# Blocks of 128 groups in all four planes, longer store rows, one load for the last V groups, and an order read from strings

## The chip, the cores and the metric

The kernel runs on one core of one Trainium2 chip. The metric is the device time of one execution in microseconds. The kernel before takes 323.43 us (median of 3 runs, 322.58 to 326.46). Profiles are of one execution, and their times count from the start of its span.

## The reference, cut to what matters

```python
q, k, v: [8, 8, 576, 64]                  # batch, heads, tokens, head_dim
q_d, k_d, v_d = means over 4 neighbouring tokens (144 groups)
out_up = repeat(softmax(q_d @ k_d.T / 8) @ v_d, 4)        # pooled attention
out_local = softmax(q @ k.T / 8 where |i - j| < 4) @ v    # banded attention
x = (out_up + out_local) as [4608, 512]   # batch * token, head * head_dim
h = x @ w_in                              # [512, 2048]
out = (h - tanh(h)) @ w_out               # [2048, 512], float32
```

Token 4g + c of a batch is plane c of group g.

## The kernel before, in words

A pair is two heads of one batch: 32 pairs, four to a batch. For each pair the kernel loads k and q (`st`, line 366), v in five overlapping windows of 128 tokens (`vst`, line 390), and for some pairs v by groups (`v4`, line 400), casts and transposes them, makes the band scores (L657, L665) and the pooled scores (L671), which use 64 rows of PE for each head, exponentials on ACT, a mask on DVE or POOL, the outs (L725), a division (L742), a transpose back and a sum of the local and the pooled part (`join`, L760). Pooled v comes for pairs 0 to 11 from products of `vw` with a selecting matrix (`pool_v`, L458), for the others from `v4` by two additions on POOL (`pool_v4`, L440, L444). The last 16 groups of k and q of all heads of a batch come in loads of their own (`sr`, line 378).

The result of a batch lies in four tiles `xT` (one per pair) of [128, 3 x 576], by plane: column c x 144 + g of a batch's slot. The dense part takes the first 512 columns of a slot, which are planes 0 to 2 and 80 groups of plane 3, as block kb (`mm1`, L803: 16 x 4 products of 128 x 512). The last 64 columns, groups 80 to 143 of plane 3, are left over; those of two batches are taken together (`left1`, L829: 4 x 16 products of 128 columns; `left2`, L855). The second product is L883 for blocks 0 to 4, and for blocks 5 to 7 a scheme of seven products in place of eight (`product`, L1030) with sums of weights (L939) and of tokens (L965, on DVE or POOL). Stores (`store`, L919) take 128 columns of the block for each of four `ts`; where such a stretch crosses from one plane to the next, it is cut in two. One row of such a store is one token's 512 values, 2 KB; for the last block 256 values.

The order of the work is a planner's (`Plan.order`): operations carry a cost in ns, a priority and the banks of PSUM that they may take, and a simulated clock puts next what can start first. A string (`GIVEN`) names the engine where there is a choice. `Plan.emit` puts filler products (L1240, on a tile of zeros) into PE gaps before the first `h` of block 1. Instructions then stand on each engine in that order and start in it.

The moving operand of a left product, before:

```python
xT[dc].rearrange("p (b c) -> p b c", c=S)[:, s0:s0 + 2, 512:S]        # line 831
```

and the one product before whose moving operand takes columns with a step (`sums`, lines 611 and 622):

```python
sel = ident.rearrange("p (g j n) -> p n g j", j=NP, n=2)[:, :, :, j]   # every 8th column
T.matmul(pl[:, :, 128:G], rr[b % 2][:, c, :], sel, start=False, stop=c == 3, ...)
```

Of the kernel before, what the change touches and what calls it, by code (L numbers as in the profile page):

```python
# [14 lines left out]
class Plan:  # L15

    LAT = {"PE": 270, "ACT": 160, "DVE": 130, "POOL": 160, "SP": 50, "DMA": 1900,
           "DW": 1900}

    def __init__(self, given):
        self.ops = []
        self.given, self.choices = given, 0
        self.last_write = {}
        self.readers = {}
        self.users = {}  # L30
        self.place = {}

    def op(self, eng, ns, fn, reads=(), writes=(), pri=0, after=0.0, slack=0.0,
           port=False, opens=None, uses=(), choice=None, rows=128, share=0.4):
# [15 lines left out]
        names = set(uses)  # L50
        if opens and not isinstance(opens, list):
            opens = [opens]
        for o in opens or ():
            names.add(o[0])
        for n in names:
            self.users.setdefault(n, []).append(i)
        if choice:

            letter = self.given[self.choices]
            self.choices += 1  # L60
            named = [a[:4] for a in choice if a[0][0] == letter]
            choice = named or [a for a in choice if len(a) == 4]
        alts = {a[0]: a for a in choice} if choice else {eng: (eng, ns, fn, port)}
        self.ops.append(dict(alts=alts, deps=deps, pri=pri, after=after, slack=slack,
                             opens=opens, names=names, rows=rows, share=share,
                             what=(list(writes) + [None])[0]))
        return i

    def order(self):
        ops, n = self.ops, len(self.ops)  # L70
        users = [[] for _ in range(n)]
        left = [0] * n
        for i, o in enumerate(ops):
            left[i] = len(o["deps"])
            for d in o["deps"]:
                users[d].append(i)
        at = [o["after"] for o in ops]
        free, ready = dict.fromkeys(("PE", "ACT", "DVE", "POOL", "SP", "DMA"), 800.0), {}
        start, engine = [None] * n, [None] * n
        pending = {k: len(v) for k, v in self.users.items()}  # L80
        ends = {}
        bank_free = [0.0] * 8
        held = [None] * 8
        port_free = 0.0
        rows = 128
        self.held = []

        def make_ready(i):
            for eng in ops[i]["alts"]:
                ready.setdefault(eng, []).append(i)  # L90

        def seats(i):
            t, got, used = 0.0, [], set()
            for _, cs in ops[i]["opens"] or ():
                best = (float("inf"), None)
                for c in cs:
                    if any(held[b] is not None or b in used for b in c):
                        continue
                    best = min(best, (max(bank_free[b] for b in c), c), key=lambda x: x[0])
                if best[1] is None:  # L100
                    return float("inf"), None
                t = max(t, best[0])
                got.append(best[1])
                used.update(best[1])
            return t, got
        for i in range(n):
            if left[i] == 0:
                make_ready(i)
        for _ in range(n):
            best = None  # L110
            for eng, cand in ready.items():
                if not cand:
                    continue
                fr = free.get(eng, 0.0)
                if eng in ("DMA", "DW"):
                    i = min(cand, key=lambda i: (at[i], i))
                    now = max(fr, at[i])
                else:
                    now, i = None, None
                    eff = []  # L120
                    for c in cand:
                        t = max(at[c], seats(c)[0], fr)
                        if ops[c]["alts"][eng][3]:
                            t = max(t, port_free)
                        eff.append((t, c))
                    now = min(eff)[0]
                    if now == float("inf"):
                        continue
                    i = min((ops[c]["pri"], c) for t, c in eff if t <= now)[1]
                if best is None or now < best[0]:  # L130
                    best = (now, eng, i)
            if best is None:
                raise RuntimeError(f"no operation can be put next: {[(e, [(ops[c].get('what'), at[c], ops[c]['opens']) for c in cs[:6]]) for e, cs in ready.items()]} {held}")
            now, eng, i = best
            for other in ops[i]["alts"]:
                ready[other].remove(i)
            o = ops[i]
            _, ns, fn, port = o["alts"][eng]
            o["fn"], o["ns"] = fn, ns
            for (name, _), c in zip(o["opens"] or (), seats(i)[1] if o["opens"] else ()):  # L140
                self.place[name] = c
                for b in c:
                    held[b] = name
                self.held.append([name, c, now, None])
            start[i], engine[i] = now, eng
            if eng == "PE":

                if o["rows"] != rows:
                    ns += 60 if rows == 128 else 95
                rows = o["rows"]  # L150
            if eng == "DMA":

                ns *= 0.89 if now > 60000 else 0.82

                slow = max(0.0, free.get("DW", 0.0) - now)
                f = o["share"]
                ns = ns / f if ns <= f * slow else ns + (1 - f) * slow
            end = now + ns
            free[eng] = end
            if port:  # L160
                port_free = end
            for name in o["names"]:
                ends[name] = max(ends.get(name, 0.0), end + self.LAT[eng])
                pending[name] -= 1
                if pending[name] == 0:
                    for b in self.place[name]:
                        held[b] = None
                        bank_free[b] = ends[name]
                    for h in self.held:
                        if h[0] == name:  # L170
                            h[3] = ends[name]
            for u in users[i]:
                same = eng in ops[u]["alts"] and len(ops[u]["alts"]) == 1 and \
                    eng not in ("DMA", "DW")
                at[u] = max(at[u], end if same else end + self.LAT[eng] + ops[u]["slack"])
                left[u] -= 1
                if left[u] == 0:
                    make_ready(u)
        self.start, self.engine = start, engine
        return sorted(range(n), key=lambda i: (start[i], i))  # L180

    def emit(self, until=None, filler=None):
        order = self.order()
        stop = min([h[2] for h in self.held if h[0] == until], default=0.0)
        last = 600.0
        for i in order:
            o = self.ops[i]
            if filler and self.engine[i] == "PE" and self.start[i] <= stop:
                gap = self.start[i] - last
                if gap > 350:  # L190
                    busy = {b for _, c, s, e in self.held for b in c
                            if s < self.start[i] and e > last - 300}
                    rest = [b for b in range(7, -1, -1) if b not in busy]
                    if rest:
                        slow = 430 if self.start[i] < 6000 else 230
                        filler(rest[0], int(0.75 * gap / slow))
                last = self.start[i] + o["ns"]
            if o["fn"] is not None:
                o["fn"]()
# [3 lines left out]
def kernel(  # L203
# [49 lines left out]
    ]  # L253

    GIVEN = (
        "..A..D.DADA.PADDADPDD.AADD..D.DD.AA.DA.ADAA....ADAD..AA..P...AP.D..AP....DDPPPDD"
        "..D..A.A...PAAAPPPAADDD.DDDDAD.ADAD.A..PPPDDDAA...A.....DA..A.AA.PD.D..ADPDDAP.P"
        "D.PP..D.DDDDD.P..DP...DADP...P....A...D.PP..DPAAPP..P.D..AD..A..DD.PPD.PA..D.P.."
# [213 lines left out]
    def attention(p):  # L472
# [248 lines left out]
        def outs():  # L721
            po = at(oname)
            for hh in range(2):
# [6 lines left out]
                for i in range(2):  # L730
                    to(1, EP + 256 * i + 128, vp[s][:, hh, i, :], False, i == 1)
# [540 lines left out]
```

## Time and profile before

| What | Value |
|---|---|
| Timed runs (3) | 323.43 us median, 322.58 to 326.46 |
| Span of the profiled execution | 320.7 us |
| Clock of TensorE granted, mean | 1.000 |
| Products on PE | 2831 |
| DMA | 59.23 MB in 117205 packets, mean 185 GB/s |

The profile gives the span of its execution, from the first to the last instruction; what lies around it in a timed run is the difference to the median, 2.7 us. PE is the matmul engine, PEld its weight loads, DVE, ACT and POOL are the vector, scalar and GpSimd engines, SP issues most DMAs. A line as L829 is a line of the kernel. A product's length in the profile holds its way through the array, in which the next ones already run: the distance from one start to the next tells the rate.

### The profile page before, as it was taken

What the parts mean: (1) busy time and instruction counts of PE and PEld (TensorE: products, weight loads), DVE (VectorE), ACT (ScalarE), POOL (GpSimd) and SP (SyncE); (2) the same over time, 40 slices, a digit from 0 to 9 for tenths busy, and PEclk for the clock granted to TensorE, in tenths of its full rate; (3) what the DMA queues carried; (4) which work ended last, traced back from release to release, by engine and by line L of the source; (5) the groups of instructions that cost most, each with busy time, mean ns of one, the idle gap of its engine ahead of it and who ended that gap; (6) DMA issues with size and microseconds to landing.
All of it is one profiled execution on the core that took longest, in us unless ns stands there. A gap on an engine that the chain in (4) does not pass through costs nothing.

```text
span 320.7 us, 7553 instructions
## 1 busy us (share of the span) xinstructions
PE 309.1 (96%) x2831; PEld 181.0 (56%) x2831; DVE 255.3 (80%) x451; ACT 207.8 (65%) x372; POOL 156.8 (49%) x185
## 2 busy tenths in 40 slices
PE   7978999999999999999999999999899999999994
PEld 3654546554754545454655444545476667666783
DVE  5685997597888898679888999899999797656853
ACT  5884995588856776369745878579766852455210
POOL 7822664326267473537464735357794653511000
PEclk9999999999999999999999999999999999999999
DMA  8999999999999999999999999995452143200414
GB/s 218 275 219 227 279 185 247 289 277 304 240 232 274 236 210 246 224 255 195 245 222 177 269 237 251 232 223 112 94 92 57 35 49 93 67 0 3 130 36 131
DMA packets 117205, 59.23 MB, mean 185 GB/s; under 512 B 85008, under 2 KB 112592, under 8 KB 117168
## 3 DMA queue, kind: packets, MB, share of 16 engines
q1 hardware_dynamic: 111584, 52.17, 71.3%
q0 software_dynamic: 4896, 5.97, 10.0%
q10 hardware_dynamic: 688, 0.61, 0.6%
q8 instruction: 22, 0.36, 0.4%
q14 instruction: 15, 0.12, 0.1%
HBM read 43.65 MB, written 9.44 MB: 166 GB/s over the span
## 4 chain that ended last, share of the span: by engine, by line
PE 88%; DMA 7%; DVE 1%; SPq 1%; ACT 0%; POOL 0%; ACTq 0%; issue 0%; POOLq 0%
PE ps L803 34%; PE ps L883 22%; PE ps L1030 11%; DMA vst<-in_v_dram 6%; PE ps L725 5%; PE ps L829 5%; PE ps L855 4%; PE ps L657 3%; DMA sr<-in_q_dram 1%; PE ps L671 1%; PE ps L510 1%; PE ps L458 1%; PE ps L767 1%; PE ps L665 1%; SPq L366 1%; DVE xT L760 1%
## 5 line engine op out<-in xcount | busy, mean ns | idle before, releaser
L803 PE MATMUL ps<-xT,w_in_sb 128*128 128x512 bf16 x512 | 124.6, 379 | 0.0
L817 DVE TENSOR_TENSOR gT<-ps,u 128x512 bf16<-128x512 f32 x128 | 86.0, 684 | 21.2 <-ACT u L814 19.6
L814 ACT ACTIVATE u<-ps 128x512 f32<-128x512 f32 x128 | 76.1, 599 | 36.2 <-PE ps L803 33.6
L883 PE MATMUL ps<-w_out_sb,gT 128*128 128x512 bf16 x320 | 78.6, 379 | 0.0
L803 PEld LDWEIGHTS <-w_in_sb 128*128 128x128 bf16 x512 | 47.1, 98 | 47.3 <-issue 0.4
L883 PEld LDWEIGHTS <-gT 128*128 128x128 bf16 x320 | 29.2, 98 | 31.2
L444 POOL TENSOR_TENSOR vp<-v 128x256 bf16<-128x256 f32 x20 | 14.6, 730 | 58.7 <-PE ps L725 48.1
L676 ACT ACTIVATE E<-ps 128x912 bf16<-128x912 f32 x32 | 29.8, 931 | 17.8 <-PE ps L665 14.6
L1030 PEld LDWEIGHTS <-gT 128*128 128x128 bf16 x288 | 27.9, 98 | 7.5
L742 DVE TENSOR_TENSOR ln<-ps,r 128x768 bf16<-128x768 f32 x32 | 30.6, 956 | 0.9
L711 DVE TENSOR_TENSOR E<-E,mask 128x1152 bf16<-128x1152 bf16 x29 | 25.6, 882 | 4.4 <-ACT E L680 4.2
L502 POOL CAST qr<-st 128x512 bf16<-128x512 f32 x32 | 22.5, 713 | 9.3 <-DMA st<-in_q_dram 6.0
L440 POOL TENSOR_TENSOR v<-v 128x512 f32<-128x512 f32 x20 | 25.4, 1271 | 1.1
L725 PEld LDWEIGHTS <-E 128*128 128x128 bf16 x576 | 21.7, 97 | 6.1
L684 ACT ACTIVATE E<-ps 128x576 bf16<-128x576 f32 x32 | 20.9, 654 | 0.0
L583 ACT COPY kt<-kq 128x576 bf16<-128x576 bf16 x16 | 18.9, 1180 | 2.9 <-DVE kq L578 2.7
L593 POOL TENSOR_TENSOR half<-kq 128x576 f32<-128x576 bf16 x13 | 18.1, 1389 | 3.6 <-DVE kq L578 1.5
L725 PE MATMUL ps<-vw,E 128*128 128x65 bf16 x320 | 18.9, 193 | 0.0
L760 DVE TENSOR_TENSOR xT<-lT 128x336 bf16<-128x336 bf16 (+1 forms) x30 | 18.4, 655 | 0.0
L1030 PE MATMUL ps<-Tw,gT 128*128 128x256 bf16 x144 | 18.3, 273 | 0.0
L725 PE MATMUL ps<-vp,E 128*128 128x65 bf16 x256 | 18.1, 193 | 0.0
L1030 PE MATMUL ps<-w_out_sb,gT 128*128 128x256 bf16 x144 | 17.8, 273 | 0.0
(118 smaller groups left out, 434.9 us busy)
## 6 DMA issues: line engine op xcount, KB each, us to landing
vst<-in_v_dram SPq DMA_DIRECT2D x64, 160.0 KB, 4.8
st<-in_k_dram SPq DMA_DIRECT2D x32, 256.0 KB, 4.6
st<-in_q_dram SPq DMA_DIRECT2D x32, 256.0 KB, 4.6
v<-in_v_dram SPq DMA_DIRECT2D x14, 256.0 KB, 3.6
w_in_sb<-in_moe_w_in_dram POOLq DMA_DIRECT2D x4, 512.0 KB, 12.7
w_out_sb<-in_moe_w_out_dram POOLq DMA_DIRECT2D x4, 512.0 KB, 12.2
out_dram<-y SPq DMA_DIRECT2D x7, 256.0 KB, 3.8
out_dram<-y SPq DMA_DIRECT2D x7, 224.0 KB, 3.1
```

The lines of the kernel that those rows point to most:

```text
L440: eng.tensor_tensor(out=v2, in0=v4[s][:, :, :, 0:128], in1=v4[s][:, :, :, 128:256], op=ALU.add)
L502: (eng, ns, lambda dst=dst, src=src, fn=fn: fn(out=dst, in_=src), port)
L676: A.activation(out=E[s][:, :, E0:E0 + 456], in_=at(s1)[:, :, PS0:512], func=AF.Exp, scale=SCALE)
L711: eng.tensor_tensor(out=el, in0=el, in1=mask.unsqueeze(1).to_broadcast([128, 2, S]), op=ALU.mult)
L725: T.matmul(po[:, hh, 65 * n:65 * n + 65], E[s][:, hh, e:e + 128], vv, start=start, stop=stop)
L742: op("DVE", 960, lambda: V.tensor_tensor(out=ln[s].rearrange("p n (h d) -> p h n d", d=D), in0=blocks()[:, :, :, 0:64], in1=r[s].unsqueeze ...
L760: eng.tensor_tensor(out=dst, in0=src, in1=add, op=ALU.add)
L803: T.matmul(at(name)[:, 0, :], w_in_sb[:, dc, fc * 128:(fc + 1) * 128], xT[dc][:, c0:c0 + 512], start=(dc == 0), stop=(dc == N_DC - 1))
L814: op("ACT", 600, lambda: A.activation(out=u[us], in_=at(name)[:, 0, :], func=AF.Tanh), reads=[("hd", kb, fc)], writes=[("u", us)], pri=-1, ...
L817: op("DVE", 690, lambda: V.tensor_tensor(out=gT[g][:, fc, :], in0=at(name)[:, 0, :], in1=u[us], op=ALU.subtract), reads=[("hd", kb, fc), ( ...
L883: T.matmul(at(name)[:, 0, :], gT[g][:, fc, ts * 128:ts * 128 + 128], w_out_sb[:, fc, :], start=(fc == 0), stop=(fc == N_FF - 1))
L1030: T.matmul(dst, left[:, f, 128 * j:128 * j + 128], right[:, f, :], start=(first and e == 0 and f == 0 and (j == 0 or apart)), stop=(e == 1 ...
```

## The change

The blocks are cut otherwise: a block is now groups 0 to 127 of all four planes, and the left-over tokens of a batch are groups 128 to 143 of all four planes, which are the last 64 tokens. The moving operand of `mm1` becomes four runs of 128 columns; that of `left1` goes through the 16 groups and, for each, over the four planes, so that the 64 tokens come out in the order of the output. A store takes 128 groups of two planes at once: a row of it is two tokens, 4 KB (for the last block 2 x 1 KB), and none is cut at a plane's end. The last 16 groups of v of all eight heads of a batch come in one load `vr` and are pooled at once into `vpr`, in which a mask (`hsel`) leaves each head its own 16 rows; `v4`, `v2` and `vp` keep the first 128 groups alone, and `pool_v` has five products for six. The pooled scores read the rows of the second half at a shifted place (`w0`). The additions of `pool_v4` may now be on DVE too.

The planner is gone. `TURNS` gives the order of all operations, `ENGINES` the engine of each choice, `BANKS` the PSUM bank of each opening and `FILL` place, bank and number of the fillers (24 in all). Costs that stand in the calls of `op` are not used any more. ACT's table is loaded by a copy of one element at the start. Cut to its core:

```diff
-    def order(self):
...
+    def emit(self, filler):
+        n = len(self.ops)
+        turn = [self.number(self.turns[2 * i:2 * i + 2]) for i in range(n)]
...
+        for i in turn:
+            fn, deps, opens, names = self.ops[i]
...
+            if i in fill:
+                b, count = fill[i]
+                filler(b, count)
+            for name, sets in opens:
+                c = self.place[name] = sets[int(next(seats))]
...
+            if fn is not None:
+                fn()
...
     def load_v4(p):
-        vv = v[b, h0:h0 + 2].rearrange("h (g c) d -> g h (c d)", c=4)
-        for i in range(2):
-            load(770 if SOFT[p] else 450,
-                 lambda i=i: (nc.gpsimd if SOFT[p] else nc.sync).dma_start(
-                     out=v4[s][0:128 - 112 * i, :, i], in_=vv[128 * i:144 - 16 * (1 - i)]),
+        load(770 if SOFT[p] else 450,
+             lambda: (nc.gpsimd if SOFT[p] else nc.sync).dma_start(
+                 out=v4[s], in_=v[b, h0:h0 + 2].rearrange("h (g c) d -> g h (c d)", c=4)[0:128]),
...
+    def load_vr(b):
+        base = v[b, 0]
+        load(500, lambda: nc.sync.dma_start(out=vr[b % 2], in_=bass.AP(
+            tensor=base.tensor, offset=base.offset + 512 * D,
+            ap=[[S * D, H], [4 * D, 16], [1, 4 * D]])),
...
+    def pool_vr(b):
...
+        def spread(eng):
+            eng.tensor_tensor(out=vpr[b % 2], in0=vrp.unsqueeze(1).to_broadcast([128, H, D + 1]),
+                              in1=hsel.unsqueeze(2).to_broadcast([128, H, D + 1]), op=ALU.mult)
...
     def pool_v(p, seats):
-            for n, (i, t) in enumerate(((0, 0), (0, 1), (0, 2), (0, 3), (0, 4), (1, 4))):
-                T.matmul(pv[:, i, :], pick[:, n, :], vw[w][:, :, t, 0:D],
-                         start=n in (0, 5), stop=n in (4, 5))
+            for t in range(NT):
+                T.matmul(at(name)[:, 0, 0:2 * D], pick[:, t, :], vw[w][:, :, t, 0:D],
+                         start=t == 0, stop=t == NT - 1)
...
     def mm1(kb, fc):
-                         xT[dc][:, c0:c0 + 512], start=(dc == 0), stop=(dc == N_DC - 1))
+                         xT[dc][:, c0:c0 + S].rearrange("p (c g) -> p c g", c=4)[:, :, 0:128],
+                         start=(dc == 0), stop=(dc == N_DC - 1))
...
     def left1(m, e):
-                             xT[dc].rearrange("p (b c) -> p b c", c=S)[:, s0:s0 + 2, 512:S],
+                             xT[dc].rearrange("p (b c g) -> p b g c", b=NR, c=4)[:, s0:s0 + 2, 128:G],
...
     def left2(m):
-            row = out[(2 * m + (n + m) % 2) * S + 4 * (G - LEFT) + 3]
+            row = out[(2 * m + (n + m) % 2) * S + 512]
-                out=bass.AP(tensor=row.tensor, offset=row.offset, ap=[[4 * Dm, LEFT], [1, Dm]]),
+                out=bass.AP(tensor=row.tensor, offset=row.offset, ap=[[Dm, LEFT], [1, Dm]]),
...
-    def store(kb, ts, ys, j, half=None, queue="SP"):
+    def store(kb, half, ys, js=(0, 1), part=None, rows=(0, 128), queue="SP"):
...
+            row = out[kb * S + 4 * r0 + 2 * half + js[0]]
+            (nc.sync if queue == "SP" else nc.scalar).dma_start(
+                out=bass.AP(tensor=row.tensor, offset=row.offset + lo,
+                            ap=[[4 * Dm, n], [Dm, len(js)], [1, hi - lo]]),
+                in_=y[ys][r0:r1, js[0]:js[-1] + 1, lo:hi])
```

More of the change, by code (lines that the diff above doesn't have):

```diff
@@ L15, with __init__, op @@
 class Plan:
-    LAT = {"PE": 270, "ACT": 160, "DVE": 130, "POOL": 160, "SP": 50, "DMA": 1900,
-           "DW": 1900}
-    def __init__(self, given):
+    DIGITS = "0123456789ABCDEFGHIJKLMNOPQRSTUVWXYZabcdefghijklmnopqrstuvwxyz"
+    def __init__(self, turns, engines, banks, fill):
         self.ops = []
-        self.given, self.choices = given, 0
+        self.turns, self.engines, self.banks, self.fill = turns, engines, banks, fill
+        self.choices = 0
         self.last_write = {}
         self.readers = {}
-        self.users = {}
         self.place = {}
-    def op(self, eng, ns, fn, reads=(), writes=(), pri=0, after=0.0, slack=0.0,
-           port=False, opens=None, uses=(), choice=None, rows=128, share=0.4):
+    def op(self, eng, ns, fn, reads=(), writes=(), port=False, opens=None, uses=(),
+           choice=None, rows=128, share=0.4):
         i = len(self.ops)
@@ L63, in op @@
[L63 to L66, printed above, removed]
-        return i
-    def order(self):
[L70 to L141, printed above, removed]
-                for b in c:
[L143 to L199, printed above, removed]
+            eng, ns, fn, port = next(a[:4] for a in choice if a[0][0] == letter)
@@ new lines, in op, with number @@
+        self.ops.append((fn, deps, opens or (), names))
+        return i
+    def number(self, text):
+        return 62 * self.DIGITS.index(text[0]) + self.DIGITS.index(text[1])
+    def emit(self, filler):
+        n = len(self.ops)
+        turn = [self.number(self.turns[2 * i:2 * i + 2]) for i in range(n)]
+        assert sorted(turn) == list(range(n))
+        fill = {self.number(f): (int(f[2]), int(f[3:])) for f in self.fill.split()}
+        left, holder = {}, [None] * 8
+        for o in self.ops:
+            for name in o[3]:
+                left[name] = left.get(name, 0) + 1
+        seats, done = iter(self.banks), set()
+        for i in turn:
+            fn, deps, opens, names = self.ops[i]
+            assert deps <= done, "an operation stands before what it needs"
+            done.add(i)
+            if i in fill:
+                b, count = fill[i]
+                assert left.get(holder[b], 0) == 0, "a bank is still in use"
+                filler(b, count)
+            for name, sets in opens:
+                c = self.place[name] = sets[int(next(seats))]
+                for b in c:
+                    assert left.get(holder[b], 0) == 0, "a bank is still in use"
+                    holder[b] = name
+            for name in names:
+                left[name] -= 1
+            if fn is not None:
+                fn()
@@ L342, in c_pick @@
         V.tensor_copy(out=pick[:, 4, 112:128], in_=group[:, 0:16])
-        V.tensor_copy(out=pick[:, 5, 0:16], in_=group[:, 16:32])
     def c_mask():
@@ L358, in load @@
     def load(ns, fn, keys, cost, pri, after=0.0, eng="SP"):
-        op(eng, ns, fn, writes=list(keys) + [("q", keys[0])], pri=pri, after=after)
-        op("DMA", cost, None, reads=[("q", keys[0])], writes=keys, pri=pri,
+        op(eng, ns, fn, writes=list(keys) + [("q", keys[0])])
+        op("DMA", cost, None, reads=[("q", keys[0])], writes=keys,
            share=0.18 if keys[0][0] == "vst" else 0.35)
@@ L428, in prep_v @@
             for eng, ns, fn, port, *more in CAST_V],
-           reads=[("vst", s, 0), ("vst", s, 1)], writes=[("vw", w)], pri=10 * p - 12,
-           after=rel)
+           reads=[("vst", s, 0), ("vst", s, 1)], writes=[("vw", w)])
     def release(p):
@@ L638, in attention @@
                                           for n, n1, _, eng in ADDERS],
-                   reads=[(key, s)], writes=[("half", m)], pri=pri)
+                   reads=[(key, s)], writes=[("half", m)])
         else:
@@ L642, in attention @@
                                       for n, n1, _, eng in ADDERS],
-               reads=[("kq", k3)], writes=[("half", 0), ("half", 1)], pri=pri)
+               reads=[("kq", k3)], writes=[("half", 0), ("half", 1)])
         if p >= NPP:
@@ L659, in score1 @@
                              start=True, stop=True)
+        w0 = [128 - 16 * (2 * j + hh) for hh in range(2)]
         def score2():
@@ L1073, in product @@
             if n == 2:
-                store(kb, 2, ya, 0, 0)
-                store(kb, 3, ya, 1, 0)
+                store(kb, 1, ya, part=0)
             if n == 6:
@@ L1081, in product @@
                 add(full[0], 5, full[1], ("keep", 1), [("keep", 0)])
-                store(kb, 0, yb, 0, 1)
-                store(kb, 1, yb, 1, 1)
+                store(kb, 0, yb, part=1)
             if n == 4:
                 plus(y[yb][:, :, 0:HD], full[2], ("keep", 2), yk(yb, 0))
-                store(kb, 0, yb, 0, 0, "ACT")
-                store(kb, 1, yb, 1, 0, "ACT")
+                store(kb, 0, yb, part=0, queue="ACT")
             if n == 3:
@@ L1092, in product @@
                         in1=full[0][:, j, :], op=ALU.add), reads=[(key, j), ("keep", 0)],
-                       writes=[("y", ya, j, 1)], pri=-1, uses=[(name, j)])
-                    store(kb, 2 + j, ya, j, 1, "SA" if j else "SP")
+                       writes=[("y", ya, j, 1)], uses=[(name, j)])
+                    if j == 0:
+                        store(kb, 1, ya, (0,), 1)
+                    else:
+                        store(kb, 1, ya, (1,), 1, (0, 64))
+                        store(kb, 1, ya, (1,), 1, (64, 128), "ACT")
             return
@@ L1111, in product @@
             if n == (3, 5)[half]:
-                for j in range(2):
-                    store(kb, 2 * half + j, ys, j)
+                store(kb, half, ys)
     def second(kb):
@@ L1179, in pads @@
                      [:, :, :, G:256], 0.0)
-        op("DVE", 500, pads, writes=[("vp", i), ("E", i, 0), ("E", i, 2), ("qkd", i)],
-           pri=-9940)
-    for i in range(NV4):
-        op("POOL", 900, lambda i=i: GP.memset(v4[i], 0.0),
-           writes=[("v4", i, 0), ("v4", i, 1)], pri=75, port=True)
+        op("DVE", 500, pads, writes=[("vp", i), ("E", i, 0), ("E", i, 2), ("qkd", i)])
+    op("POOL", 700, c_hsel, writes=["hsel"], port=True)
+    op("DVE", 70, lambda: V.memset(vrp[:, D:D + 1], 4.0), writes=["vrp"])
     load_qk(0)
     load_rest(0)
+    load_vr(0)
     for p in range(NP):
```

337 lines of the change are left out of this document (199 added, 138 removed).

## The prediction

> **What bounds the kernel now.** I read the page's shares and slices first, then the busy time by stage, the waits of PE, and last the timeline of PE alone, product by product.
>
> ```profile
> PE 309.1 (96%) x2831; PEld 181.0 (56%) x2831; DVE 255.3 (80%) x451; ACT 207.8 (65%) x372; POOL 156.8 (49%) x185
> ...
> PE   7978999999999999999999999999899999999994
> ...
> PEclk9999999999999999999999999999999999999999
> DMA  8999999999999999999999999995452143200414
> ```
>
> PE is busy in every slice but the first four, one at 224 us and the last. The clock row is full throughout, so no time is to be had from the clock. DMA is as full as PE up to 216 us, so the stages tell which of the two is waited for:
>
> ```profile
> 0.00:24.00 24.00, 18.94 (x264) 12.96 (x265) 16.09 (x54) 18.22 (x37) 15.02 (x27) 1.00 1.08 238
> ...
> 32.00:224.00 192.00, 192.00 (x1677) 101.19 (x1674) 163.93 (x287) 139.06 (x249) 103.00 (x122) 1.00 1.05 236
> 224.00:232.00 8.00, 7.03 (x54) 3.26 (x51) 7.62 (x12) 6.75 (x11) 6.25 (x8) 1.00 0.43 94
> 232.00:312.00 80.00, 80.00 (x735) 56.16 (x735) 59.64 (x85) 39.88 (x69) 30.41 (x26) 1.00 0.27 56
> ```
>
> Columns are stretch, length, then busy time of PE, PEld, DVE, ACT, POOL, the clock, DMA share and GB/s. PE has 192.00 of 192.00 us and 80.00 of 80.00 us: DMA, DVE, ACT and POOL are all covered by it. The waits of PE are few:
>
> ```profile
> PE ps L458 <- POOL vw L427: 2.0, 3, 1.4
> PE ps L534 <- POOL rr L492: 1.6, 1, 1.6
> ...
> PE ps L829 <- DVE gT L817: 1.0, 1, 1.0
> ```
>
> Busy alone does not say that PE is at its rate, so I added up the distances from each product's start to the next one's. At the rates seen when nothing waits, L803 is 512 x 0.2156 = 110.4 us, L883 69.0, L1030 336 x 0.109 = 36.7, L855 13.8, L829 256 x 0.0558 = 14.3, L725 about 17, scores, transposes and the rest 29: 290.1 us. The 19 filler products (L1240), with what is waited behind them, are 8.5 us, the 88 changes between 64-row and 128-row products 8.5, other waits and small delays 7.9, 1.3 us stand before the first product and 4.5 from the last one's start to the end of the last store. That is the span, 320.7 us. All but about 13 us of waits and fillers, nearly all of them before 33 us, is PE's own work, so **a microsecond added to a PE product is a microsecond of time**, wherever it stands after 33 us.
>
> **The change, part by part.**
>
> *The 64 tokens left over in each batch (L829).* Before, the moving operand takes two runs of 64 neighbouring columns of xT (line 831). After, it takes groups 128 to 143 of all four planes in the order group, plane: the inner step goes over the four planes, 144 elements apart, so that no two columns that follow each other are neighbours. 256 products are of this kind, of 128 columns each. The trace has one product with such an operand: L622, whose moving operand is every eighth column of the identity (line 611), 32 columns. Beside it, what L829 costs now:
>
> ```profile
> 9.54 0.61 PE L619 MATMUL ps<-ident,qr 128*128 128x128 bf16 x8
> 9.99 0.40 PE L622 MATMUL ps<-ident,rr 128*128 128x32 bf16 x4
> 10.21 0.40 PE L1240 MATMUL ps<-lT 128*128 128x512 bf16 x1
> ```
>
> ```profile
> 85.25 1.96 PE L829 MATMUL ps<-xT,w_in_sb 128*128 128x128 bf16 x32
> 87.04 0.59 PE L883 MATMUL ps<-w_out_sb,gT 128*128 128x512 bf16 x2
> ```
>
> Columns are start, length, what. 32 products of 128 columns in short runs take 87.04 - 85.25 = 1.79 us, 56 ns each. Four products of 32 stepped columns take 10.21 - 9.99 = 0.22 us, 55 ns each: as long for 32 columns as for 128. It isn't the weights, which change at each product in L725 too, at 30 ns a product; nor adding to the same place, which L725 does as well. So 128 stepped columns should take what four L622 take, 222 ns, and L829's successor 256 x (222 - 56) = **+42.5 us**. The price for a step of 144 elements is not in the trace, only that for 8. From below: if L622's surplus (55 ns against 32/128 of the column rate, 13 ns) is a fixed cost of a product, 128 columns take 53 + 42 = 96 ns, +10.2 us. From above: the later three of the four stand 60 ns apart, which makes 240 ns, +47 us. Below nothing is excluded: nothing is read less often. I take 222 ns, since a cost per column is what a change of operand alone can bring, and L829 differs from L622 in size and step only.
>
> [...]
>
> *The blocks (L803).* Each of 512 products now reads four runs of 128 columns, 144 apart, in place of one run of 512. Runs are free in this trace: L829's two runs of 64 go at 56 ns, what 128 columns of a transpose (L619) take, and L657 reads four runs of 28 at 49 ns a pair. I take 0; for bounds, a seam of 1 ns more or less at three seams a product is 1.5 us either way.
>
> *V pooled from vw (L458).* Five products of 128 columns in place of six, in 12 pairs: 12 x 56 ns = -0.7 us on PE.
>
> *Order from strings.* The order of instructions shows 70 changes between 64-row and 128-row products, 88 before. One costs 0.1 us: three L803 from 99.81 end their share at 100.46 and L657 starts at 100.55; after it four L803 take 0.97 us where 0.86 would do.
>
> ```profile
> 99.81 0.81 PE L803 MATMUL ps<-xT,w_in_sb 128*128 128x512 bf16 x3
> 100.55 0.38 PE L657 MATMUL ps<-kq,kt 64*128 64x112 bf16 x8
> 100.86 1.04 PE L803 MATMUL ps<-xT,w_in_sb 128*128 128x512 bf16 x4
> 101.83 0.23 PE L665 MATMUL ps<-kq,kt 64*128 64x120 bf16 x2
> ```
>
> 18 x 0.096 = -1.7 us. The wait at 230 us (L829 for gT, 1.1 us in start distances) goes: PE reaches each later point 10 us later or more, and DVE, which it waited for, has less to do; -1.1 us. In the opening stretch SP now issues k and q of pairs 0 to 2 before any vst, and the 24 fillers (19 before) stand elsewhere. What is late next there is vw for the pooling and the first outs, as at 29 us now, since the vst loads move behind k and q of pairs 1 and 2, and the new vr load stands among them. Of the 13 us that this stretch loses, bounds +2 (five more fillers at 0.4 us) and -4 (the waits of 1.6 and 2.0 us and some fillers); I take -1.0.
>
> *Last V groups in one load, stores of 4 KB rows.* SP issues 237 rows of instructions for 283: the 16-row loads go (14 on SP, 6 on POOL), 8 vr loads come, and 59 stores of y become 18. At 0.6 us of SP each that is much queue time, but PE waits for no store before the end, and for loads only in the opening stretch: 0. Cover: PE's 272 us without a gap. At the end the last store is 64 rows on SP and 64 on ACT, for 48 and 80 now: 0 to -0.3; I take 0.
>
> *DVE, ACT, POOL.* POOL loses half of L440 and L444 (40.0 us to about 14) and two memsets (1.8), but is given 8 masks for 3 (2.4 us each), 13 joins for 5 (1.6), 9 wide or narrow token sums for 1 (4.1 for the wide), 21 casts of vw for 11 (0.7), and the spreading of vr. I come to about 205 us for POOL, 233 for DVE, 195 for ACT in 360 us. All stay under PE, which now gives them 12% more time: 0. If that cover fails, see rival 3.
>
> Sum on the span: 320.7 + 42.5 - 0.7 - 1.7 - 1.1 - 1.0 = 358.7 us. The three timed runs are 322.58, 323.43 and 326.46 us, the median 2.7 above this span, so **361.4 us**.
>
> **The rivals.**
>
> 1. *The step is free* (the side of no loss). Everything else stands: 320.7 - 4.5 + 2.7 = 318.9 us. Place: the 256 products alone. [...] For it: L829's present runs cost nothing. Against it: L622. The point from which it decides: 2% of 323.4, about what a measurement of this kernel can tell from no change, is 6.5 us; with the 4.5 us gained, the extra must stay under 11 us, 43 ns a product. So anything over 99 ns a product is slower.
> 2. *The surplus is fixed* for each product, 96 ns: 318.9 + 10.2 = 329.1 us, just within 2%. For it: L622 is one size only, so the trace can't part a fixed cost from one per column. Against it: no other group of small products has such a cost (L725, 65 columns, 30 ns).
> 3. *POOL becomes what PE waits for.* A wide token sum on POOL takes 4.07 us (one L965 on POOL) for 1.28 to 1.39 on DVE, and six of them now stand before products L1030 in the last 80 us. If the first product behind each waits for the difference, 6 x 2.7 = +16 us at worst; the slower L829s between them make room, so +3 to +6 is likelier: 365 to 367 us.
> 4. *The strings don't pay*: PE waits in the opening or at the block borders by some us more than now: 361.4 + 4.5 + 2 = 368.
>
> **How the numbers follow.** Forecast with its own spread (216 to 240 ns, -4 to +2 in the opening): 73%, 356 to 367 us. Rivals 3 and 4: 8%, 365 to 377. A price between 100 and 200 ns: 7%, 330 to 355. Rival 1: 9%. Rival 2: 3%. The range 345 to 370 us leaves out rivals 1 and 2, most of the price in between and the upper end of 3, just under 2 in 10. Faster by over 2% needs rival 1 and more than 2 us beyond its 4.5: 2%. Within 2%: the rest of rival 1 and most of rival 2: 9%. Slower: 89%.
>
> **What would show it.** L829's successor: 32 products in a row that take 7.1 us for 1.79, and busy time of that line near 60 us for 16.6. L803's successor still 216 ns apart. PE near 349 us busy, no gap at 230. If that line keeps 56 ns, the forecast is wrong by its one large term; if PE's waits hold more than 5 us after 33 us, rival 3 or 4 is true beside it.

## The result, and the profile after

The changed kernel takes 378.45 us (median of 4 runs, 377.47 to 380.18), the kernel before 324.11 us beside it (4 runs, 322.58 to 326.46): 1.167 times as long, 95% interval 1.161 to 1.173. The forecast was 361.4 us with a range of 345 to 370. Direction and main mechanism are as forecast; the time lies 8 us above the range. The profiled execution took 378.9 us, its span 377.2.

The page of the kernel after, its shares and slices:

```profile
PE 364.0 (96%) x2824; PEld 201.7 (53%) x2824; DVE 236.7 (63%) x429; ACT 197.3 (52%) x358; POOL 202.0 (54%) x237
...
PE   8888999999999999999999999999999999999995
...
PEclk9898999999579999996899999999799999998799
DMA  8999999969914999999339999553413220200123
...
L807 PE MATMUL ps<-xT,w_in_sb 128*128 128x128 bf16 x256 | 60.7, 399 | 0.0
```

PE is as full as before. New is the clock row: it was 9 in all slices, and now it is 5 to 8 in nine of them. The busy time of the left product, L807 (L829 before), is 60.7 us; near 60 was forecast. The stages of the kernel after (stretch, length, busy time of PE, PEld, DVE, ACT, POOL, granted clock, DMA share, GB/s):

```profile
24.00:32.00 8.00, 5.45 (x92) 3.91 (x89) 7.11 (x19) 6.25 (x15) 4.73 (x7) 1.00 1.16 239
...
88.00:96.00 8.00, 8.00 (x52) 4.24 (x49) 4.76 (x11) 3.39 (x7) 6.93 (x11) 0.87 1.01 223
96.00:104.00 8.00, 8.00 (x53) 4.81 (x50) 1.19 (x3) 2.63 (x5) 5.87 (x5) 0.50 1.04 245
176.00:184.00 8.00, 8.00 (x30) 3.47 (x28) 4.67 (x8) 5.32 (x7) 5.29 (x7) 0.71 0.67 202
224.00:232.00 8.00, 8.00 (x54) 3.69 (x53) 3.07 (x7) 2.93 (x5) 5.02 (x7) 1.00 1.15 241
```

At 96 us PE is busy for 8.00 of 8.00 us, and the granted clock is 0.50. The gap at 230 us is gone. PE alone in two of these stretches (start, length, what):

```profile
87.43 2.32 PE L780 MATMUL ps<-xT,w_in_sb 128*128 128x512 bf16 x10
89.59 1.95 PE L807 MATMUL ps<-xT,w_in_sb 128*128 128x128 bf16 x8
91.36 0.47 PE L439 MATMUL ps<-vw,pick 128*128 128x128 bf16 x5
91.66 3.73 PE L807 MATMUL ps<-xT,w_in_sb 128*128 128x128 bf16 x16
95.33 0.56 PE L633 MATMUL ps<-kq,kt 64*128 64x112 bf16 x8
```

```profile
174.72 1.74 PE L807 MATMUL ps<-xT,w_in_sb 128*128 128x128 bf16 x7
176.29 3.35 PE L861 MATMUL ps<-w_out_sb,gT 128*128 128x512 bf16 x8
179.48 1.72 PE L807 MATMUL ps<-xT,w_in_sb 128*128 128x128 bf16 x7
```

Eight L807 take 91.36 - 89.59 = 1.77 us, 221 ns each; ten L780 with their four runs of 128 take 2.16 us, 216 each, as before. But eight L861 of 512 columns, with which the change does nothing, take 179.48 - 176.29 = 3.19 us for the 1.73 of their usual rate: from the second on they start 426 ns apart. The waits of PE (total, times, longest):

```profile
PE ps L703 <- DVE E L689: 3.3, 5, 0.9
PE ps L1210 <- DVE lT L1132: 1.3, 1, 1.3
PE ps L489 <- POOL qr L482: 0.9, 1, 0.9
PE ps L439 <- DVE vw L408: 0.8, 1, 0.8
```

Adding up the distances from start to start, as the prediction did, gives PE's account. The last column is an experiment told below, the changed kernel with the left products reading whole runs.

| Part of the span, us | before | after | whole runs |
|---|---|---|---|
| Products at their usual rate | 290.1 | 290.1 | 289.8 |
| Surplus of the left products | 0.1 | 42.5 | 0.7 |
| Other products at half clock | 0 | 11.3 | 1.1 |
| Waits | 5.8 | 10.8 | 14.6 |
| Fillers | 8.5 | 9.1 | 8.4 |
| Changes between 64 and 128 rows | 8.4 | 6.4 | 6.4 |
| Small delays, before the first and after the last product | 7.8 | 7.0 | 7.1 |
| Span | 320.7 | 377.2 | 328.1 |

(In the trace of the last column, `a_plain`, 26 rows of products are missing; 0.216 us for each is counted as products and not as waits.) Of the 56.4 us more (differences taken before rounding), 42.4 are the surplus of the stepped operand, 11.3 are products of other lines at half clock, 4.9 are waits, 0.5 fillers; the changes of rows give back 2.0, the rest 0.8.

### The profile page after: what moved, and what is told of

Its sections match the earlier page's. It is cut to its first block, busy times and chain, and to the rows that moved or that the text cites. A ratio compares the mean times of both kernels' runs of the same rounds, so it can differ in the third digit from the quotient of the medians.

```text
span 377.2 us, 7436 instructions
## 1 busy us (share of the span) xinstructions
PE 364.0 (96%) x2824; PEld 201.7 (53%) x2824; DVE 236.7 (63%) x429; ACT 197.3 (52%) x358; POOL 202.0 (54%) x237
## 4 chain that ended last, share of the span: by engine, by line
PE 55%; DVE 6%; issue 1%; ACT 0%; DVEq 0%; ACTq 0%
PE ps L780 15%; PE ps L861 12%; PE ps L807 11%; PE ps L1001 10%; PE ps L703 2%; PE ps L833 2%; DVE gT L795 2%; DVE E L689 1%; PE ps L633 1%; DVE qr L482 1%; DVE vw L408 0%; ACT u L792 0%; PE ps L649 0%; DVE Tw L910 0%; DVE ln L721 0%
## 5 line engine op out<-in xcount | busy, mean ns | idle before, releaser
L780 PE MATMUL ps<-xT,w_in_sb 128*128 128x512 bf16 x512 | 127.8, 382 | 0.5 <-DVE gT L795 0.5
L792 ACT ACTIVATE u<-ps 128x512 f32<-128x512 f32 x128 | 73.1, 600 | 50.2 <-PE ps L780 43.4
L861 PE MATMUL ps<-w_out_sb,gT 128*128 128x512 bf16 x320 | 84.5, 397 | 0.0
L780 PEld LDWEIGHTS <-w_in_sb 128*128 128x128 bf16 x512 | 48.0, 98 | 51.9 <-issue 2.6
L807 PE MATMUL ps<-xT,w_in_sb 128*128 128x128 bf16 x256 | 60.7, 399 | 0.0
L861 PEld LDWEIGHTS <-gT 128*128 128x128 bf16 x320 | 30.8, 102 | 35.5 <-issue 5.3
L807 PEld LDWEIGHTS <-w_in_sb 128*128 128x128 bf16 x256 | 29.1, 116 | 25.6 <-issue 1.0
L482 POOL CAST qr<-st 128x512 bf16<-128x512 f32 x38 | 25.1, 671 | 9.6 <-DMA st<-in_k_dram 4.5
L818 ACT ACTIVATE u<-ps 128x512 f32<-128x512 f32 x16 | 9.5, 597 | 38.9 <-PE ps L807 38.8
L739 POOL TENSOR_TENSOR xT<-lT 128x336 bf16<-128x336 bf16 (+1 forms) x26 | 19.0, 751 | 19.3 <-DMA lT<-ln 19.3
L575 POOL TENSOR_TENSOR qkd<-half 128x288 bf16<-128x288 f32 x22 | 19.3, 879 | 13.9 <-PE ps L780 7.6
L820 DVE TENSOR_TENSOR gL<-ps,u 128x512 bf16<-128x512 f32 x16 | 10.9, 688 | 23.2 <-ACT u L818 23.2
L689 DVE TENSOR_TENSOR E<-E,mask 128x1152 bf16<-128x1152 bf16 x24 | 22.0, 918 | 3.0 <-ACT E L658 1.6
```

The source lines that it names most:

```text
L482: (eng, ns, lambda dst=dst, src=src, fn=fn: fn(out=dst, in_=src), port)
L689: eng.tensor_tensor(out=el, in0=el, in1=mask.unsqueeze(1).to_broadcast([128, 2, S]), op=ALU.mult)
L780: T.matmul(at(name)[:, 0, :], w_in_sb[:, dc, fc * 128:(fc + 1) * 128], xT[dc][:, c0:c0 + S].rearrange("p (c g) -> p c g", c=4)[:, :, 0:128 ...
L792: op("ACT", 600, lambda: A.activation(out=u[us], in_=at(name)[:, 0, :], func=AF.Tanh), reads=[("hd", kb, fc)], writes=[("u", us)], uses=[n ...
L807: T.matmul(at(name)[:, 0, 128 * f:128 * f + 128], w_in_sb[:, dc, (f0 + f) * 128:(f0 + f) * 128 + 128], xT[dc].rearrange("p (b c g) -> p b ...
L861: T.matmul(at(name)[:, 0, :], gT[g][:, fc, ts * 128:ts * 128 + 128], w_out_sb[:, fc, :], start=(fc == 0), stop=(fc == N_FF - 1))
```

## The experiments

My theory after the result: the step costs four times the column rate in each left product (221 ns for 56), and behind a run of such products the granted clock falls to 0.50 for those that follow. The rivals: the step costs only the 42 us and the clock falls for another reason (the new order); or order and layout, not the step, are what costs.

**The step taken out of the changed kernel** (`a_runs16`). PE reads the 64 tokens by plane, in runs of 16; DVE puts them in the order of the output as it writes gL.

```diff
-                             xT[dc].rearrange("p (b c g) -> p b g c", b=NR, c=4)[:, s0:s0 + 2, 128:G],
+                             xT[dc].rearrange("p (b c g) -> p b c g", b=NR, c=4)[:, s0:s0 + 2, :, 128:G],
...
-            out=gL[:, f0:f0 + 4, :],
-            in0=at(name)[:, 0, :].rearrange("p (f c) -> p f c", c=128),
-            in1=u[us].rearrange("p (f c) -> p f c", c=128), op=ALU.subtract),
+            out=gL[:, f0:f0 + 4, :].rearrange("p f c -> p (f c)").rearrange("p (x g c) -> p x c g", g=16, c=4),
+            in0=at(name)[:, 0, :].rearrange("p (x c g) -> p x c g", c=4, g=16),
+            in1=u[us].rearrange("p (x c g) -> p x c g", c=4, g=16), op=ALU.subtract),
```

> The changed kernel, with one edit: the left product reads its 128 columns plane by plane, in eight runs of 16 neighbours, and the subtraction on DVE that writes gL puts them back in the order group, plane. Order strings, stores and loads as changed. Theory (the step costs 167 ns a product, and stretches full of such products let the granted clock fall): products 56 ns apart in place of 223, 42.5 us less; the low-clock stretches at 94, 172, 183, 268 and 347 us are gone and about 9 us with them; those at 15 and 32 us, which come from the opening, stay; 378.5 - 51 = 327 us. Rival (the clock falls for the sake of the new order): the stretches after 90 us stay, 336 us. Rival (16 neighbours are still dear): over 340 us.

Measured: 330.77 us (329.94 to 332.94), 1.022 times before (1.014 to 1.029). The group of L807 and of DVE's L820 in this kernel (busy, mean ns of one, idle before):

```profile
L807 PE MATMUL ps<-xT,w_in_sb 128*128 128x128 bf16 x256 | 18.0, 219 | 1.9 <-DVE gL L820 1.9
...
L820 DVE TENSOR_TENSOR gL<-ps,u 128x512 bf16<-128x512 f32 x16 | 20.1, 1306 | 0.4 <-ACT u L818 0.4
```

The distance is 56 ns again, and every stretch of half clock after 40 us is gone; one of 3.4 us at 33 us stays. So the step, undone alone, gives back 48 us, more than its 42.5. I had expected 327 us; the kernel is still some 7 us above the one before.

**The step put into the kernel before** (`b_step16`). The moving operand goes through the same 64 columns with an inner step of 16 elements (32 bytes), order and stores untouched; DVE's L842 puts them back, at 2.34 us for 0.68.

```diff
-                             xT[dc].rearrange("p (b c) -> p b c", c=S)[:, s0:s0 + 2, 512:S],
+                             xT[dc].rearrange("p (b c) -> p b c", c=S)[:, s0:s0 + 2, 512:S].rearrange("p b (a j) -> p b j a", j=16),
...
```

> The kernel before, with one edit: the left product reads the same 64 + 64 columns with an inner step of 16 elements (32 bytes, four at a time), and DVE puts them back when it writes gL. Planner, order, stores as before. Theory: 223 ns a product, so the price does not depend on how long the step is (16 bytes in the identity product, 288 bytes in the change, 32 here), and low clock in the stretches where 24 to 40 such products stand in a row: 324 + 42.5 + 6 to 9 = 372 to 376 us, with the clock full up to 80 us. Rival (the clock fell because of the new order): 366 us and clock 1.000. Rival (the long step is what costs): well under 223 ns and under 355 us.

Measured: 378.56 us (377.23 to 379.35), 1.168 times before (1.160 to 1.175), 3 us over the expected 372 to 376. The distance is 223 ns, the surplus 42.7 us, and 11.3 us of other products run at half clock, in five stretches, each behind left products; none is in the opening. The clock row of its page:

```profile
PEclk9999999998599999998579999999559999997599
```

The step alone, in the old order, makes both the surplus and the low clock. That the new order lowers the clock is refuted for the four borders; in the opening it is not, as there are no left products before 40 us.

**The same products set apart, with a control** (`b_step16_apart`, `b_apart`). In both the left products stand between the products of the block, in groups of 8 to 16, in place of a run at its end; `b_apart` has no step.

```diff
...
-                else:
-                    left1(kb // 2, i - 16)
+                if kb % 2 and i < 16 and i % 4 == 1:
+                    halves = left1(kb // 2, i // 4)
+                    next(halves)
+                if kb % 2 and i < 16 and i % 4 == 3:
+                    next(halves, None)
```

> As b_step16, but the planner is given the left products between the block's products, eight or sixteen in a row with four to sixteen wide ones between, in place of all at the block's end. Theory (the granted clock answers to stretches of some 3.4 us that hold almost nothing but stepped reads): still 223 ns a product, but a clock of 0.99 or more: the control b_apart + 42.5 us. Rival (the clock answers to the amount of stepped reads in all): clock as in b_step16, control + 49 to 52 us.

> Control: the kernel before with the left products between the block's products as in b_step16_apart, read in runs as before. Both theories: clock 1.000, the time of the kernel before give or take 4 us, for the order alone.

Measured: 377.34 us (377.24 to 379.02) with the step, 329.33 (three runs, 326.60 to 329.61; 1.012 times before, 1.001 to 1.024) without. The 48.0 us between them lie between what I expected (42.5) and the rival (49 to 52). I expected the clock to be full; it was 0.977, and 7.6 us of half clock were left, in five stretches of 3.41 us. The one at 20 us, in the opening, is not behind left products. Behind left products the clock falls four times (71, 92, 102 and 269 us), and each time two groups of eight stood together: 16 stepped products in a row, 3.6 us. Three other rows of 16 (at 79, 178 and 258 us) and all the single eights keep the clock. The control was to have a full clock too and has one stretch at half, at 282 us; it follows 3.4 us in which PE waited for `xT` (L803, 2.3 and 1.1 us). So in this run half clock also stands behind a wait.

**Never more than eight in a row** (`b_step16_eight`). One more dependency keeps the two halves of a group apart, and a group now starts one product of the block earlier (`i % 4 == 0` for 1):

```diff
-                reads=[("w_in", e)] + [("xs", s0 + i, j) for i in range(2) for j in range(N_DC)],
+                reads=[("w_in", e)] + [("xs", s0 + i, j) for i in range(2) for j in range(N_DC)] +
+                [("hd", 2 * m + 1, 4 * e + 3 * n)],
...
```

> As b_step16_apart, but never more than eight stepped products in a row: each half of a left group waits for the block product ahead of it. Theory (the clock is granted by windows of 3.41 us, and halves after a window in which products take in columns less than about 0.37 of the time): eight stepped products and four wide ones make 0.48, so no low clock after the opening, less than 1.5 us of slow products, still 223 ns a stepped product; 324 + 42.5 + 2 to 8 for the order = 369 to 374 us. Rival (the clock answers to the amount of stepped reads): 7 to 11 us of slow products as before, 377 us or more.

Measured: 370.75 us (370.14 to 372.83). Surplus 42.2 us, half clock 1.1 us, in one stretch at 315 us behind a wait of PE's for `xT` of 2.1 us. Three borders of this kernel by stage, the clock in the third column from the end:

```profile
86.00:97.00 11.00, 11.00 (x71) 5.20 (x69) 7.89 (x13) 6.50 (x12) 1.70 (x3) 1.00 0.76 178
172.00:184.00 12.00, 12.00 (x84) 6.01 (x83) 10.22 (x17) 7.18 (x11) 4.88 (x6) 1.00 0.77 141
264.00:276.00 12.00, 12.00 (x103) 6.56 (x102) 10.81 (x16) 7.29 (x14) 1.58 (x2) 1.00 0.30 56
```

The same number of the same products costs 6.6 us less than in `b_step16_apart`, and the half clock is 6.5 us less. Of the 7.6 us there, the stretch in the opening can hold at most 1.7, half its length; the rest, behind stepped products, goes to nothing. So the clock's part is parted from the surplus. It also bears on what goes ahead of a fall. In the trace of the kernel after, each stretch at one clock between 5.2 and 377.2 us is a multiple of 3.41 us long, the low ones 3.41, 6.83 or 13.65 us. I took the share of each such 3.41 us (a window, below) in which products take in columns, as an estimate: from the rates of 512 and 128 columns (215.6 and 55.8 ns), 128 columns take (215.6 - 55.8) / 384 x 128 = 53 ns, so a stepped product counts with 53 of its 223 ns. In that trace the five windows behind which the clock falls at the borders of the blocks (from 90.5, 169.0, 179.3, 264.6 and 343.1 us) have 0.29 to 0.34. Two windows have some 0.39: behind the one at 29.1 us, in the opening, the clock falls, behind the one at 274.8 us it stays. At half clock the window at 346.5 us has 0.70 to 0.72 and the clock stays low; the next one, 0.74 to 0.77, ends it. The shares move by some 0.02 with where the window is set against the step of the clock, so the border, some 0.39, is an estimate. Stepped products alone make 53 / 223 = 0.24: the window at 179.3 us, where PE is busy for all of the 3.41 us, has 0.29, and the clock behind it is 0.50.

**How small a step is free** (`b_step2`, `b_step4`, `b_step8`). As `b_step16`, with `j=2`, `4` and `8`: 4, 8 and 16 bytes from one column to the next.

> As b_step16 with an inner step of 2 elements (4 bytes). Theory A (a column read by itself costs four times a column read with its neighbour, whatever the step): 223 ns. [...]

> The kernel before, with the moving operand of L829 stepped by four elements (8 bytes) within each 64 columns, and DVE putting the columns back as it writes gL. [...] A price that is there or not: 57 ns and 325 us, or 223 ns and 375 to 380 us.

> As b_step16 with an inner step of 8 elements (16 bytes), the step of the identity product. [...] A price that grew with the step would be lower here than at 32 bytes.

Measured: 324.65 us (8 runs, ratio 1.0005, 0.996 to 1.005), 340.22 (2 runs, 1.044, 1.035 to 1.054) and 379.65 (2 runs, 1.170). L829 in the three kernels, in that order:

```profile
L829 PE MATMUL ps<-xT,w_in_sb 128*128 128x128 bf16 x256 | 16.9, 218 | 1.0 <-DVE gT L817 1.0
```

```profile
L829 PE MATMUL ps<-xT,w_in_sb 128*128 128x128 bf16 x256 | 32.1, 295 | 1.0 <-DVE gT L817 1.0
```

```profile
L829 PE MATMUL ps<-xT,w_in_sb 128*128 128x128 bf16 x256 | 59.5, 400 | 1.0 <-DVE gT L817 1.0
```

From start to start: 57 ns, 117, 223, and 223 with a step of 32 bytes as with the change's 288. It doubles with the step up to 16 bytes and then stays: 0.45 ns a column at 4 bytes, 0.91 at 8, 1.74 at 16, 32 and 288. Why it does is not shown. `b_step4` keeps its clock after the opening (0.992 over the span), in accord with the windows: 53 / 117 = 0.45 is above the 0.39.

**What is left without the step** (`a_runs16_rows`, `a_plain`). The 48 us that the runs of 16 gave back left the kernel 7 us above the one before. First, whether DVE's dearer L820 (1306 ns for 688) holds PE up: gL stays by plane, and the store of the 64 tokens is cut into four of 16 rows.

> The changed kernel with the left product read in runs of 16 as in a_runs16, but gL is left in that order, and the store of a batch's 64 rows is cut in four of 16 rows, one for each plane (32 stores for 8). So DVE's 16 subtractions are short again (0.69 us for 1.31). If a_runs16 was slower than the kernel before for DVE's sake: 324 us or less. If it was for the order of the strings, most of all in the opening: 327 to 330 us.

Measured: 336.63 us (336.24 to 337.50), 1.038 (1.031 to 1.044): slower than what it was to mend. L820 is back at 682 ns, but PE has a new wait:

```profile
PE ps L807 <- DVE gL L820: 5.3, 1, 5.3
```

The queue of SP ahead of it:

```profile
150.08 2.12 SPq L851 DMA_DIRECT2D out_dram<-keep  x4
152.30 0.40 SPq L324 DMA_DIRECT2D st<-in_q_dram  x1
152.81 1.26 SPq L533 DMA_TRANSPOSE kq<-qr  x1
```

SP now issues 32 stores for 8. DVE waits 7.3 us for a transpose of k and q issued behind them, and L820 stands behind on DVE. But the two transposes are issued no later than in `a_runs16` (152.8 and 155.5 us for 153.5 and 156.4): late is the landing. The first lands 8.7 us after its issue, where the longest in `a_runs16` takes 5.9, and DVE goes on behind the second at 165.2 us, there at 162.4. That the small stores are the cause is likely and not shown. So this run can't decide about DVE; it shows that an order written for one set of transfers can lose more by a change to the stores than was to be won. Second, with DVE and the stores untouched (`a_plain`), the left products read two runs of 64. These are the columns that the kernel before left over; the kernel leaves out that the left-over tokens are now others:

```diff
-                             xT[dc].rearrange("p (b c g) -> p b g c", b=NR, c=4)[:, s0:s0 + 2, 128:G],
+                             xT[dc].rearrange("p (b c) -> p b c", c=S)[:, s0:s0 + 2, 512:S],
```

> The changed kernel, with L807 reading two runs of 64 neighbouring columns (columns 512 to 575 of each slot, as before); everything else, DVE's subtraction too, as in the changed kernel. It leaves out that these columns are the left-over tokens: the left products are of other tokens than the output needs. My theory: the step costs 42.5 us by itself and some 9 us of the 11.3 us of slow clock, so 378.5 - 42.5 - 9 = 327 us, 325 to 329, 1.00 to 1.02 of the kernel before; L807 at 56 ns, waits of PE near 10 us as in the changed kernel, the clock full after 40 us. The rival, that the order from strings costs nothing and the 330.8 us of the runs of 16 were DVE's dearer subtraction (16 x 0.62 us = 10 us): 319 to 321 us. The other rival, that new layout and order cost 7 us or more by themselves: 330 us or more.

Measured: 330.68 us (329.80 to 331.61) beside 325.67 for the kernel before on that chip: 1.016 (1.009 to 1.023). The ratio is in the expected 1.00 to 1.02, the time 1.7 us above 329 and over the 330 us of the second rival: layout and order cost something by themselves, 5.0 us by the medians. The first rival (319 to 321 us) is refuted. `a_runs16` took 330.77 us, 1.022 of its own before; the intervals overlap. DVE's dearer subtraction (16 x 0.62 us) shows in the time with some 2 us (0.6%) by the middle values; the intervals allow anything from nothing to about 5 us. In its one profile PE waits 1.9 us for L820, here 0.7. Clock row and waits of PE of this kernel:

```profile
PEclk9997999999999999999999999999999999999998
```

```profile
PE ps L703 <- DVE E L689: 4.0, 4, 1.1
PE ps L489 <- DVE qr L482: 1.7, 2, 1.6
PE ps L1210 <- DVE lT L1132: 1.3, 1, 1.3
PE ps L649 <- DVE qkd L575: 1.1, 1, 1.1
PE ps L780 <- DVE gT L795: 1.1, 1, 1.1
```

Without the step the change costs 328.1 - 320.7 = 7.4 us between these two profiles (the one of before is of one of its shortest executions), and by the account that is 8.8 us more of waits and 1.1 of half clock, less 2.0 for changes of rows and 0.5 of the rest. Layout and stores are not seen in it: L780 keeps 216 ns, and no wait of PE's is put down to a store. The waits have no single source (some ten of up to 1.6 us, in the opening and at the borders of the blocks, for masks, casts and subtractions that come late). Not all of them need be the order: `b_step2`, with the old order and nothing dearer on PE, has 8.8 us of waits in its one profile where before has 5.8.

## Why the prediction was wrong in size, step by step

- **Stepped left products, +42.5 us (222 ns each)**: right. 42.4 us, 223 ns. Four columns' time for each column, read from 16 small products (L622), held for ones four times as wide and for a step of 288 bytes for one of 16. The second had no row behind it and was luck: the price grows up to a step of 16 bytes, L622's, and only there stops (117 ns in `b_step4`, 223 in `b_step8` and `b_step16`). Rivals 1 (free) and 2 (a fixed surplus) are refuted.
- **"The clock row is full throughout, so no time is to be had from the clock"**: this step failed. It is true of the kernel before and says nothing of a kernel whose products take four times as long for the same columns. It cost 11.3 us, and no rival had it; without them the time would lie within the range. The sign "PE near 349 us busy" failed with it: 364.0 us. The numbers for the question were in the prediction: 32 left products in a row at 222 ns are 7.1 us with a quarter of the columns. That the granted clock falls to 0.50 while PE is busy throughout, behind windows in which products took columns for 0.29 to 0.34 of the time, could not be read from the trace of before, which has no such stretch and no low clock. About 2.5 of the 11.3 us stand before 40 us, where no left product is; there the products come between waits, and `a_plain` also has one such stretch (1.1 us), without any stepped left product.
- **Order from strings, -1.7 us for 18 changes of rows**: right, -2.0.
- **The wait at 230 us, -1.1 us**: right in its place, wrong as a saving. It is gone, and from 33 us on PE waits 4.5 us for 1.2 before, in other places, just under the 5 us that were to be the sign of rivals 3 and 4.
- **The opening, -1.0 us, bounds +2 and -4**: wrong beyond its bounds. Waits before 33 us are 6.3 us for 4.6, fillers 0.5 more, half clock 2.5: +4.7. Together with the last point, waits and fillers are +5.4 us where the sum had -2.1. This was rival 4 ("the strings don't pay", 4.5 + 2 us), and `a_plain` shows it larger than it gave: without the slow left products the waits are 8.8 us above before. That the other engines catch up while PE is slow is the likely reason; no run parts it.
- **Runs of 128 at nothing, stores and loads at nothing, DVE, ACT and POOL under PE**: right. L780 keeps 216 ns; POOL is busy 202.0 us (about 205 forecast), DVE 236.7 (233), ACT 197.3 (195). Rival 3, POOL as the bound, is not seen: no wait of PE's for POOL is over 0.9 us.
- **Pick, -0.7 us**: the 12 products are gone; the sum of the products at their rate, 290.1 us in both, is not fine enough to show it.

Of the span, 377.2 - 358.7 = 18.5 us were missed: 11.3 the clock, 7.5 waits and fillers (+5.4 for -2.1), and the small terms take back 0.3. What lies around the span was taken as 2.7 us and is 1.7 in the profiled execution: the median of before had been set beside the span of a shorter execution.

What stays open: which of the late operations in the opening and at the borders is the first cause of the waits. There is no run with the old planner's order and the new blocks, and none with an order made for the runs of 16. Of the versions tried, none beats the kernel before.

## What to carry to other kernels

In these runs a step in PE's moving operand was priced by the bytes between columns that follow each other: a product of 128 bf16 columns took 56 ns without a step, 57 at 4 bytes, 117 at 8 and 223 at 16, 32 and 288. So reorder in a layout, or on an engine with room (16 dearer writes of DVE's, 9.9 us in all, cost some 2 us here by the middle values, and not more than about 5), and keep runs for PE. When a change makes PE's products slower, look at the granted clock too: in the kernel after it fell to 0.50 behind windows of 3.41 us in which products took columns for less than about four tenths of the time (an estimate), and in `b_step16_apart` eight slow products between full ones kept the clock where sixteen in a row lost it four times in seven. A written order fits one set of durations and queue times; every edit to an operation in it is also an edit to the waits.

## What was not expected of the hardware

- PE at 100% busy in the profile was granted 0.50 of the clock (96 to 104 us of the kernel after), behind stepped products that took 223 ns for the 56 without a step.
- At half clock stepped products keep their 223 ns while products on whole rows go from 216 to 426: the time of the stepped read did not follow the granted clock.
- DVE's price for writing 512 bf16 values with a step (subtraction into gL): 682 ns without (before), 728 with a step of 4 bytes (`b_step2`), 1298 to 1306 with 8 (`b_step4`, `a_runs16`), 2430 with 16 (`b_step8`) and 2342 with 32 (`b_step16`). Of the 16 x 1.66 = 26.6 us more in `b_step16`, 2 us at most show: its span is 55.9 us longer, and the surplus and the half clock are 54.0 of them.
